# Denominators in the score banks, V's copies on VectorE and no moving product: one edit to the forward recurrence of a fused training step

## The chip, the cores and the metric

The program runs on one core of a Trainium2 chip. The core has a matrix engine (TensorE, in the profile "PE" for its products and "PEld" for its weight loads), a vector engine (VectorE, "DVE"), a scalar engine (ScalarE, "ACT"), GpSimd ("POOL") and SyncE ("SP"), which here only issues DMAs. Each engine works through its own list of instructions in order; semaphores hold an instruction back until what it needs is there. Sums of the matrix engine land in PSUM, which this kernel uses as eight banks; everything else lives in SBUF, or in the chip's memory, which DMAs reach.

The metric is the device time of one execution in microseconds. Before the edit it is 3096.96 us, the median of three runs (3095.86 to 3097.39).

## The reference

The kernel computes a transformer block and all its gradients. The part that matters here is the forward pass of the attention, which is a recurrence over 64 segments of 32 rows: eight memory rows go in front of each segment, and the first eight rows of a segment's output are the memory of the next.

```python
for s in range(n_seg):                       # 64 segments, one after the other
    h = jnp.concatenate([mem, xs], axis=1)   # 8 + 32 rows of 512
    q = jnp.einsum('btd,dhe->bhte', h, Wq)   # 32 heads of 128
    k = jnp.einsum('btd,dhe->bhte', h, Wk)
    v = jnp.einsum('btd,dhe->bhte', h, Wv)
    scores = jnp.einsum('bhqe,bhke->bhqk', q, k) * scale
    scores = jnp.where(mask[None, None], scores, -1000000000.0)
    p = _softmax(scores, axis=-1)
    o = jnp.einsum('bhqk,bhke->bhqe', p, v)
    o = jnp.einsum('bhte,hed->btd', o, Wo)
    mem = o[:, :M, :].copy()                 # the next segment needs it
    outs.append(o[:, M:, :])
```

Around it stand layer norms with a modulation, a gated feed-forward part, and `jax.vjp` over the whole.

## The kernel before, in words

`phase2` is the forward recurrence, a Python loop over `s` from 0 to 63 that writes out one step for each segment. Everything in it is put in the order in which it is traced: `self.pin` at the end of the phase ties each instruction to the one before it on its engine, so the order of the lines is the order on every engine. The backward pass, the feed-forward part and the weight gradients follow in other phases and are not touched.

Three heads are worked on at once: their 3 x 40 rows make 120 columns of a 128-wide group, and 32 heads make `G` = 11 groups. Groups go in three parts of four, four and three (`PG` = 4): "part 0, 1, 2".

A step goes like this:

- `proj` (L692) makes K, Q and V rows of the segment, each in two halves of 16 products of 128x512 (`col_pass`, L255). VectorE copies the first half out of PSUM, ScalarE the second; V's halves are both copied by VectorE, to `RA["v"]`, which is named RA0v in the profile.
- `turns` (L701) transposes K and Q on the matrix engine; VectorE and ScalarE put them head by head into `kT` and `qT`.
- V's rows have to be moved into `Vst`, group by group. Two copies by GpSimd bring the first 1024 columns (L794 for the first half, L797 for the second). The heads of partitions 96 to 127 ("far heads") have to move to partitions 0 to 95. That is `vshift` (L736): three products with a piece of the identity into a bank `sh_ps`, and a VectorE copy from there (L743). V's rows for the memory arrive by DMA from `RBv`, issued by GpSimd a step ahead (`v_tails`, L671).
- `st_exp` (L710) makes the scores of a part in a bank of their own (`st_ps`; the mask was put there before by `mask_mm`, L658), and ScalarE exponentiates them into `ET` (L717).
- `den` (L719) multiplies `ET` with a column of ones: the softmax's denominators. They are put into the unused fourth quarter of the bank `or2`, which later takes part 2 of the output. `recip` (L724) inverts them on VectorE into `rden`, parts 0 and 1 in one instruction, part 2 in another.
- `pv` (L745) multiplies `ET` with `Vst` into `or_ps`. `ost` (L754) scales by `rden` into `Ost`: parts 0 and 2 on VectorE, part 1 on ScalarE in four pieces.
- `ott` (L765) transposes `Ost` on the matrix engine; the copies to `OT` are ScalarE's for parts 0 and 2, VectorE's for part 1.
- `outproj` (L769, products on L223 through `pair_mm`) applies the output weights in 64 products, heads in order, so its first product needs part 0 of `OT` alone. Its sum is split, folded (`at_ft`) and put into the next step's `hT` (L875).

Two of the transposes that the backward pass needs are made by DMA: `VTr` from `Vst` (L814) and `Pst` from `ET` (L820), both on SP's queue, which also carries all stores of rows. At the start of the next step `norm` (L884) scales `Pst` on GpSimd and SP stores `VTr` and `Pst` (L887, L888).

Steps come in fours, since rows of four segments are prepared together. Between the scores and the output a step also holds: in the first of four a modulation product (`mod_ps`, L200), in the second nothing, in the third the transpose of the prepared K rows (`turn_ps`, L618), in the fourth that of the Q rows and a transpose of new input rows (`p1tp`, L415, with a ScalarE copy `hx`, L417). In the text these are the "mod", "plain", "k-turn" and "q-turn" steps. Each step also puts three `mask_mm` of the next step among its transposes.

PSUM has two pools: three banks for `st_ps`, five for everything else ("p").

Of the kernel before, what the change touches and what calls it, by code (L numbers as in the profile page):

```python
# [40 lines left out]
class K:  # L41
# [392 lines left out]
    def phase2(self):  # L434
# [4 lines left out]
        PG = 4  # L439
# [8 lines left out]
        with ExitStack() as ctx:  # L448
# [232 lines left out]
            for s in range(NS):  # L681
# [27 lines left out]

                def st_exp(pi):  # L710
                    st_ps = masked.pop(pi)
# [7 lines left out]
                def den(pi, ps):  # L719
                    for g in range(pi * PG, min(pi * PG + PG, G)):  # L720
                        nc.tensor.matmul(ps[:, PG - 1, g:g + 1], lhsT=ET[:, g * GW:(g + 1) * GW], rhs=self.ones[:, 0:1],
                                         start=True, stop=True)

                def recip(a, b, ps):  # L724
                    a, b = a * PG, min(b * PG, G)
                    nc.vector.reciprocal(rden[:, a:b], ps[0:120, PG - 1, a:b])
# [9 lines left out]
                def vshift():  # L736
                    sh = ps_f32("sh_ps")
                    shf = sh[:].rearrange("p g x -> p (g x)")
                    for hl in range(3):
                        nc.tensor.matmul(shf[32 * hl:32 * hl + 32, 0:384], lhsT=self.ident[96:128, 96:128],  # L740
                                         rhs=RA["v"][96:128, 384 * hl:384 * hl + 384], start=True, stop=True,
                                         tile_position=(96, 32 * hl))
                    nc.vector.tensor_copy(Vst[0:96, 1024:1408], shf[0:96, 0:384])  # L743

                def pv(pi, or_ps=None):  # L745
                    or_ps = or_ps or ps_f32("or_ps")
# [7 lines left out]
                def ost(pi, or_ps, eng):  # L754
                    n = min(PG, G - pi * PG)
                    if eng == "act":
                        for j in range(n):
# [4 lines left out]
                    nc.vector.tensor_tensor(part3(Ost, pi)[0:120, 0:n, :], or_ps[0:120, 0:n, :],  # L762
                                            rden[:, pi * PG:pi * PG + n].unsqueeze(2).to_broadcast([120, n, 128]), op=ALU.mult)

                def ott(pi):  # L765
                    ps, n = transposes_part(Ost, pi)
                    self.evac("dve" if pi == 1 else "act", part3(OT, pi)[:, 0:n, :], ps)
# [9 lines left out]
                if s < NS - 1 and norms:  # L777
                    norms.pop()()
                proj("k", 0, "dve")
                proj("k", 1, "act")  # L780
                if s == NS - 1:
                    nc.gpsimd.dma_start(self.w_gate, io["B_w_gate"].rearrange("(c p) f -> p c f", p=128))
                    norms.pop()()
# [11 lines left out]
                turns()  # L795
                proj("v", 1, "dve")
                nc.gpsimd.tensor_copy(Vst[0:96, 512:1024], RA["v"][0:96, 512:1024])  # L797
# [13 lines left out]
                vshift()  # L811
                st_exp(2)
                if s < NS - 1:
                    nc.sync.dma_start(VTr[:], Vst[:, :], transpose=True)  # L814
                or2 = ps_f32("or_ps")
                den(0, or2)
                or0 = pv(0)
                Pst = sb2.tile([128, G, 128], BF16, name="Pst", bufs=1)
                if s < NS - 1:
                    nc.sync.dma_start(Pst[:], ET[:, :], transpose=True)  # L820
                else:
                    nc.gpsimd.dma_start(self.w_up, io["B_w_up"].rearrange("(c p) f -> p c f", p=128))
                    nc.gpsimd.dma_start(self.w_down, io["B_w_down"].rearrange("(fc p) d -> p fc d", p=128))
                den(1, or2)
                or1 = pv(1)
                recip(0, 2, or2)
                ost(0, or0, "dve")
                ost(1, or1, "act")
                pv(2, or2)
                den(2, or2)  # L830
# [1307 lines left out]
```

The softmax here doesn't subtract the row's maximum and nothing guards it: scores larger than these inputs give would overflow.

## Time and profile before

| | |
|---|---|
| time, median of 3 runs | 3096.96 us |
| the profiled execution | 3095.76 us, of which its span is 3093.9 us |
| forward recurrence | its hand-over copies to the next step (L875) run from 62.8 to 980.5 us of the span |
| one step (from one `at_ft` to the next) | mod 15.04, plain 14.59, k-turn 14.70, q-turn 14.93 us; 14.82 us on average |
| TensorE's granted clock | 0.991; 1.00 in the recurrence |

How to read it: the page gives each engine's busy time and the chain of work that ended last. A step is best read in the timeline of one window: its columns are the start in us, the length in us, the engine, the line, the operation, output <- input, how often, and in brackets how long the engine was idle before and on what it waited. Instructions of one line that stand together are drawn as one row. Products are pipelined and their ends are modelled, so their lengths overlap, and a busy matrix engine says little.

### The profile page before, as it was taken

How to read it: one execution, taken by the hardware profiler on the slowest of the kernel's cores; microseconds unless marked ns; L12 is line 12 of the kernel's file. 1: busy time of each engine (PE TensorE's matmuls, PEld its weight loads, DVE VectorE, ACT ScalarE, POOL GpSimd, SP SyncE). 2: the span in 40 equal slices, each digit the busy share in tenths (PEclk: the TensorE clock that was granted, in tenths of full speed). 3: DMA queues.
4: the chain of work that ended last, by engine and by line, in shares of the span. 5: the costliest groups of instructions: out<-in, count | busy, mean ns of one | idle time of the engine just before them, and what ended most of it. 6: DMA issues, size and time to landing. Idle time of an engine off the chain costs nothing.

```text
span 3093.9 us, 106049 instructions
## 1 busy us (share of the span) xinstructions
PE 2997.4 (97%) x43769; PEld 1835.7 (59%) x43845; DVE 1628.3 (53%) x3799; ACT 1269.5 (41%) x3056; POOL 1378.6 (45%) x2958
## 2 busy tenths in 40 slices
PE   5999999999999899989999999999999999999999
PEld 3666666666665444445577777777777754445454
DVE  4556656665555788742255555555555642322221
ACT  2555555555555433322255555555555530111011
POOL 3666766666766222211244444444444422333322
PEclk8999999999999899999999999999999999999999
DMA  9887788788788799997599999999999998666574
GB/s 299 217 213 203 205 206 216 201 213 211 206 201 255 200 231 232 224 284 247 170 239 243 245 243 244 239 248 244 244 240 245 245 271 279 195 201 220 190 237 148
DMA packets 845944, 703.54 MB, mean 227 GB/s; under 512 B 544306, under 2 KB 717906, under 8 KB 845076
## 3 DMA queue, kind: packets, MB, share of 16 engines
q1 hardware_dynamic: 714148, 486.69, 62.3%
q0 software_dynamic: 60656, 148.64, 14.9%
q10 hardware_dynamic: 70656, 61.41, 6.4%
q8 instruction: 345, 5.65, 0.8%
q14 instruction: 139, 1.14, 0.1%
HBM read 294.93 MB, written 276.35 MB: 185 GB/s over the span
## 4 chain that ended last, share of the span: by engine, by line
PE 90%; DMA 4%; DVE 3%; issue 1%; POOL 1%; ACT 1%; SPq 0%; another core or an unknown queue 0%; DVEq 0%; POOLq 0%; ACTq 0%
PE pass_ps L255 18%; PE gps L1928 13%; PE dh_ps L215 8%; PE g_ps L1590 6%; PE gps5o L1942 4%; PE at_ps L223 4%; PE dhq_ps L223 4%; PE gps L1277 3%; PE mm L1121 3%; PE dh_tps L215 3%; PE turn_ps L264 2%; PE dp_ps L1569 2%; PE tps L1502 2%; PE tps L733 2%; PE mm L1081 2%; DVE RA0v L63 1%
## 5 line engine op out<-in xcount | busy, mean ns | idle before, releaser
L1928 PE MATMUL gps<-rows,hrows 128*128 128x512 bf16 (+2 forms) x2124 | 415.6, 355 | 1.9
L1928 PEld LDWEIGHTS <-hrows 128*128 128x128 bf16 x2160 | 211.2, 98 | 204.6
L255 PEld LDWEIGHTS <-hT 128*32 128x32 bf16 x6144 | 158.2, 97 | 161.3 <-issue 1.9
L1634 POOL COPY dOst<-RAd 96x512 bf16<-96x512 bf16 x128 | 75.4, 612 | 312.2 <-DVE RAd L63 312.2
L63 DVE CAST ot<-gps 128x512 bf16<-128x512 f32 (+3 forms) x76 | 48.1, 633 | 274.8 <-PE gps L1928 185.8
L1932 POOL DMA_DIRECT2D out_dram<-ot x108 | 81.3, 753 | 248.9 <-DVE ot L63 136.5
L61 ACT ACTIVATE ot<-gps 128x512 bf16<-128x512 f32 (+3 forms) x75 | 41.3, 551 | 349.5 <-PE gps L1928 221.7
L885 POOL TENSOR_TENSOR Pst<-Pst,rden 120x1408 bf16<-120x1408 bf16 x63 | 159.6, 2533 | 43.8 <-issue 28.4
L61 ACT ACTIVATE dVT<-g_ps 128x512 bf16<-128x512 f32 (+1 forms) x192 | 109.5, 570 | 95.3 <-PE g_ps L1590 95.0
L63 DVE CAST RA0v<-pass_ps 128x512 bf16<-128x512 f32 x128 | 88.5, 692 | 89.4 <-PE pass_ps L255 85.5
L215 PE MATMUL dh_ps<-WvT,dVT 128*32 128x512 bf16 x2048 | 133.4, 380 | 0.2 <-DVE RBd L63 0.2
L255 PE MATMUL pass_ps<-Wv,hT 128*32 128x512 bf16 x2048 | 133.3, 380 | 0.0
L1942 PE MATMUL gps5o<-WoT,rows 128*128 128x512 bf16 x580 | 127.8, 379 | 3.9 <-DMA rows<-OSR 3.2
L255 PE MATMUL pass_ps<-Wk,hT 128*32 128x512 bf16 x2048 | 123.3, 383 | 1.5 <-ACT hT L875 1.1
L1579 DVE SCALAR_TENSOR_TENSOR dS<-dp_ps,Pst_l 128x512 bf16<-128x512 f32 (+1 forms) x192 | 112.1, 640 | 22.1 <-PE dp_ps L1577 22.1
L223 PE MATMUL at_ps<-Wo,OT 128*32 128x256 bf16 x4096 | 123.5, 273 | 0.1
L255 PE MATMUL pass_ps<-WoT,dyT 128*32 128x256 bf16 (+1 forms) x3072 | 122.4, 308 | 0.9 <-ACT dyT L1708 0.9
L223 PE MATMUL dhq_ps<-WqT,dQT 128*32 128x256 bf16 x4096 | 122.9, 273 | 0.0
L215 PE MATMUL dh_ps<-WkT,dKT 128*32 128x512 bf16 x2048 | 122.2, 380 | 0.0
L255 PE MATMUL pass_ps<-Wq,hT 128*32 128x512 bf16 x2048 | 121.6, 379 | 0.0
L223 PEld LDWEIGHTS <-dQT 128*32 128x32 bf16 x4096 | 109.6, 97 | 15.9
L717 ACT ACTIVATE ET<-st_ps 128x480 bf16<-128x480 f32 (+1 forms) x192 | 96.0, 535 | 42.6 <-ACT qT L61 34.7
(419 smaller groups left out, 7082.2 us busy)
## 6 DMA issues: line engine op xcount, KB each, us to landing
OSR<-Ost SPq DMA_DIRECT2D x64, 352.0 KB
OT<-OT SPq DMA_DIRECT2D x64, 352.0 KB
VT<-VTr SPq DMA_DIRECT2D x64, 352.0 KB
PS<-Pst SPq DMA_DIRECT2D x64, 352.0 KB
OT_l<-OT SPq DMA_DIRECT2D x64, 352.0 KB
Pst_l<-PS SPq DMA_DIRECT2D x64, 352.0 KB
VT_l<-VT SPq DMA_DIRECT2D x64, 352.0 KB
DVR<-rows_x POOLq DMA_DIRECT2D x64, 352.0 KB, 6.4
```

The lines of the kernel that those rows point to most:

```text
L61: return nc.scalar.activation(out, in_, AF.Copy)
L63: return nc.vector.tensor_copy(out, in_)
L215: self.nc.tensor.matmul(ps[32 * j:32 * j + 32, :], lhsT=lhsT, rhs=w, start=(n < 4), stop=(n >= total - 4), tile_position=(0, 32 * j))
L223: nc.tensor.matmul(ps[32 * j:32 * j + 32, :], lhsT=x[k], rhs=w[k][:, 256 * d:256 * d + 256], start=(n == 0), stop=(n == total - 1), tile_p ...
L255: self.nc.tensor.matmul(ps[32 * j:32 * j + 32, :], lhsT=lhs(c), rhs=rhs, start=(c == 0), stop=(c == DC - 1), tile_position=(0, 32 * j))
L717: nc.scalar.activation(part3(ET, pi)[:, 0:n, 0:120], st_ps[:, 0:n, 0:120], AF.Exp, scale=cfg.scale)
L885: nc.gpsimd.tensor_tensor(Pst[0:120, :, :], Pst[0:120, :, :], rden[:, :].unsqueeze(2).to_broadcast([120, G, 128]), op=ALU.mult)
L1121: nc.tensor.matmul(hp[:], lhsT=xT[:, fc, :], rhs=wT[:, fc, :], start=(n == 0), stop=(n == 2 * FC - 1))
L1579: nc.vector.scalar_tensor_tensor(out=part3(dS, pi), in0=ps[:, 0:n, :], scalar=cfg.scale, in1=part3(Pst, pi), op0=ALU.mult, op1=ALU.mult)
L1590: nc.tensor.matmul(ps[:, j, :], lhsT=lh[:, g * GW:(g + 1) * GW], rhs=rh[:, g * GW:(g + 1) * GW], start=True, stop=True)
L1928: nc.tensor.matmul(ps[:, 0:ng * E], lhsT=hrows[:, tp_, c * 128:(c + 1) * 128], rhs=rows[:, tp_, 0:ng * E], start=(tp_ == 0), stop=(tp_ == ...
L1942: nc.tensor.matmul(pss[gg][:], lhsT=src[0][:, src[1], gg * E:(gg + 1) * E], rhs=dyrows[:, tp_, :], start=(tp_ == order[0]), stop=(tp_ == o ...
```

## The change: what it does

1. The denominators of part `pi` are written into columns 120 to 123 of that part's own score bank, which the scores leave free, instead of into `or2`. `recip` becomes three instructions, one for each part, and the next step's `mask_mm` of a bank now follows it.
2. `vshift` is removed. Its place is taken by `far`, which copies V's far heads directly from `RA["v"][96:128]` on VectorE: two copies (32x384 and 32x128) after the first half of V, two (32x256 each) after the second.
3. The copy of V's second half into `Vst` moves from GpSimd to VectorE.
4. The DMA transpose of `ET` to `Pst` is issued ahead of that of `Vst` to `VTr`; both stand behind part 0 of `pv`.
5. The modulation product and the transposes of the prepared rows are put between the scores and the first `den`.
6. `ost` of part 0 is cut into two VectorE instructions of two groups, around `recip` and `ost` of part 1. `OT` of parts 0 and 2 is copied by VectorE, of part 1 by ScalarE, and the three `mask_mm` stand around part 0's transpose.
7. In the last step `norm` is put behind V's copies; the store of `Pst` is returned as a function of its own and is called at once.

The diff, cut to its core:

```diff
-                def den(pi, ps):
+                def den(pi):
                     for g in range(pi * PG, min(pi * PG + PG, G)):
-                        nc.tensor.matmul(ps[:, PG - 1, g:g + 1], lhsT=ET[:, g * GW:(g + 1) * GW], rhs=self.ones[:, 0:1],
+                        j = 120 + g - pi * PG
+                        nc.tensor.matmul(sts[pi][:, 0, j:j + 1], lhsT=ET[:, g * GW:(g + 1) * GW], rhs=self.ones[:, 0:1],
                                          start=True, stop=True)
-                def recip(a, b, ps):
-                    a, b = a * PG, min(b * PG, G)
-                    nc.vector.reciprocal(rden[:, a:b], ps[0:120, PG - 1, a:b])
+                def recip(pi):
+                    a, n = pi * PG, min(PG, G - pi * PG)
+                    nc.vector.reciprocal(rden[:, a:a + n], sts[pi][0:120, 0, 120:120 + n])
...
-                def vshift():
-                    sh = ps_f32("sh_ps")
-                    shf = sh[:].rearrange("p g x -> p (g x)")
+                def far(hf, engs):
                     for hl in range(3):
-                        nc.tensor.matmul(shf[32 * hl:32 * hl + 32, 0:384], lhsT=self.ident[96:128, 96:128],
-                                         rhs=RA["v"][96:128, 384 * hl:384 * hl + 384], start=True, stop=True,
-                                         tile_position=(96, 32 * hl))
-                    nc.vector.tensor_copy(Vst[0:96, 1024:1408], shf[0:96, 0:384])
+                        lo, hi = max(384 * hl, 512 * hf), min(384 * hl + 384, 512 * hf + 512)
+                        if lo < hi:
+                            self.evac(engs.pop(0), Vst[32 * hl:32 * hl + 32, 1024 + lo - 384 * hl:1024 + hi - 384 * hl],
+                                      RA["v"][96:128, lo:hi])
...
                 turns()
+                far(0, ["dve", "dve"])
                 proj("v", 1, "dve")
-                nc.gpsimd.tensor_copy(Vst[0:96, 512:1024], RA["v"][0:96, 512:1024])
+                nc.vector.tensor_copy(Vst[0:96, 512:1024], RA["v"][0:96, 512:1024])
+                far(1, ["dve", "dve"])
+                if s == NS - 1:
+                    norms.pop()()()
...
                 st_exp(0)
                 st_exp(1)
-                vshift()
                 st_exp(2)
-                if s < NS - 1:
-                    nc.sync.dma_start(VTr[:], Vst[:, :], transpose=True)
-                or2 = ps_f32("or_ps")
-                den(0, or2)
-                or0 = pv(0)
...
-                den(1, or2)
-                or1 = pv(1)
-                recip(0, 2, or2)
-                ost(0, or0, "dve")
-                ost(1, or1, "act")
-                pv(2, or2)
-                den(2, or2)
-                recip(2, 3, or2)
-                ost(2, or2, "dve")
...
                 fill(s4, "turn")
+                den(0)
+                or0 = pv(0)
+                Pst = sb2.tile([128, G, 128], BF16, name="Pst", bufs=1)
+                if s < NS - 1:
+                    nc.sync.dma_start(Pst[:], ET[:, :], transpose=True)
+                    nc.sync.dma_start(VTr[:], Vst[:, :], transpose=True)
...
+                recip(0)
+                ost(0, or0, "dve", 0, 2)
+                den(1)
+                or1 = pv(1)
+                recip(1)
+                ost(1, or1, "act")
+                ost(0, or0, "dve", 2, 4)
                 if s4 == 3:
                     p1(s // nseg_t + P1_AHEAD, 4)
...
+                den(2)
+                or2 = pv(2)
+                recip(2)
+                ost(2, or2, "dve")
                 if more:
                     mask_mm(more.pop(0))
+                ott(0, "dve")()
+                while more:
+                    mask_mm(more.pop(0))
+                o1 = ott(1, "act")
+                o2 = ott(2, "dve")
+                o1()
+                o2()
```

## The prediction, made before the changed kernel was run

> **What bounds the kernel now.** I read the page first for its shares, then the chain of waits through the recurrence, then the timeline of single steps. The page alone would say that the matrix engine is all there is:
>
> ```profile
> PE 2997.4 (97%) x43769; PEld 1835.7 (59%) x43845; DVE 1628.3 (53%) x3799; ACT 1269.5 (41%) x3056; POOL 1378.6 (45%) x2958
> ```
>
> The chain of waits in a plain step shows where the time between V's last product and the output products goes (start, length, what):
>
> ```profile
> 604.13 0.70 DVE RA0v L63
> 604.84 0.04 issue
> 604.88 0.34 PE sh_ps L740 x2
> 605.22 0.26 PE st_ps L715 x3
> 605.48 0.08 PE or_ps L721 x4
> ...
> 605.92 0.22 DVE rden L726
> ...
> 608.19 1.87 PE at_ps L223 x64
> ```
>
> The matrix engine stands still while VectorE copies V's second half, because two products of `vshift` and then the scores of part 2 stand behind that copy. From the start of that copy (I call it e0) to the first output product this step takes 608.19 - 604.13 = 4.06 us. The same two pieces give 4.51 in the mod step (648.62 to 653.13), 4.18 in a k-turn step (678.25 to 682.43) and 4.34 in a q-turn step (633.70 to 638.04). Only this stretch is changed; the rest of a step (10.5 us) is left as it is. The timeline shows who is late in it:
>
> ```profile
> 603.54 0.28 DVE L63 COPY qT<-turn_ps 128x64 bf16<-128x64 bf16 x2
> 604.13 0.69 DVE L63 CAST RA0v<-pass_ps 128x512 bf16<-128x512 f32 x1 [0.31 <-PE pass_ps L255]
> 604.41 1.63 ACT L717 ACTIVATE ET<-st_ps 128x480 bf16<-128x480 f32 x3 [0.55 <-ACT qT L61]
> ...
> 605.25 0.55 DVE L743 CAST Vst<-sh_ps 96x384 bf16<-96x384 f32 x1 [0.42 <-PE sh_ps L740]
> ...
> 605.92 0.21 DVE L726 RECIPROCAL rden<-or_ps 120x8 f32<-120x8 f32 x1
> 606.16 0.69 DVE L762 TENSOR_TENSOR Ost<-or_ps,rden 120x512 bf16<-120x512 f32 x1
> 606.29 1.14 ACT L759 ACTIVATE Ost<-or_ps,rden 120x128 bf16<-120x128 f32 x4 [0.25 <-PE or_ps L750]
> ```
>
> ScalarE's exponentials end at 606.04 whatever the matrix engine does (three in a row, from 604.41). Its scaling of part 1 starts at 606.29, ends at 607.43, and the transposes of parts 1 and 2 and the output follow from there. So the quantity to follow is: when does ScalarE start the scaling of part 1? Now the matrix engine sets it, by 0.25 us.
>
> **What the skill says.** Four places, the last of them with the cost that it bears on. *Trainium Kernel Development and Optimization*, section Performance Expectations: matmul busy time is a bad metric of how near the roofline a kernel is. The trace agrees: 97% on the page beside the standstill above. *VectorE: DVE Perf Modes*, The perf-mode tier table: a copy from SBUF to SBUF in bf16 runs at four elements a cycle. The trace has such copies (L277): 1536 columns 0.556 us, 1024 columns 0.421 us, so 0.26 ns a column and 0.156 us fixed. The same page, Two Vector instructions with no wait between them: an instruction whose input or output starts in another group of 32 partitions than that of the one before is held until all earlier ones have finished. The trace agrees where partitions 96 and 0 alternate:
>
> ```profile
> 1000.93 0.69 DVE L897 TENSOR_TENSOR Pst<-tps,rden 120x512 bf16<-120x512 bf16 x1
> 1001.65 0.43 DVE L896 COPY Pst<-tps 32x512 bf16<-32x512 bf16 x1
> 1002.12 0.69 DVE L897 TENSOR_TENSOR Pst<-tps,rden 120x512 bf16<-120x512 bf16 x1
> ```
>
> Each starts 0.03 us after the end of the one before, while instructions on the same partitions overlap (the three of L277 at 28.10 take 1.36 us together, 1.53 one by one: 0.085 us overlap).
>
> **The change part by part**, in the plain step above.
>
> *Out:* `vshift`'s products and the standstill. The scores of part 2 follow those of part 1 at once, some 0.8 us earlier. But exponentials are paced by ScalarE (604.41 to 606.04) and start with part 0, so no `ET` comes earlier. L743's 0.55 us on VectorE and L797's 0.61 on GpSimd go. GpSimd's time is free here: its Vst DMAs come earlier and are for the next step. So this edit alone gives the matrix engine time, and 0.25 us of it can be used before ScalarE's scaling.
>
> *In, on VectorE.* Each of the new copies changes its group of 32 partitions in input or output, so I take no overlap and 0.03 us between two. V's copies to the first reciprocal, with the fit above for copies: the far copies of the first half start at 603.85, behind qT: 0.255 and 0.19, to 604.32. V's second half is thus copied from 604.35 (now 604.13) to 605.04; `Vst` 0.29 to 605.36; two far copies of 0.22 to 605.86; reciprocal of part 0 (0.17, as L726 on three columns) to 606.06; half of `ost` part 0, 256 columns: L762 takes 0.691 for 512 and 0.557 for 384, so 0.42, from 606.09 to 606.52; the reciprocal of part 1 begins 0.08 before that ends, as L726 does now at 606.77, and ends at 606.61. ScalarE starts at 606.66 instead of 606.29. **VectorE is 0.37 us later than the matrix engine was.** It ends part 1 at 607.80.
>
> *Behind it.* Now the mask products, and ScalarE's copy of part 0, which waits behind the scaling, delay the output products to 608.19, 0.76 after the scaling's end. After, masks and turns are done by then, part 0 is copied by VectorE (second half of `ost` to about 606.95, reciprocal, part 2 to 607.63, copy 0.42 to 607.97), and only one transpose of part 1, three of part 2 and one or two others follow: 0.06 to start, then 0.067 us each (four weight loads take 0.27 at 607.49), and the first output product at about 608.31. Part 1's copy on ScalarE (608.2 to 608.8) is needed after 24 of 64 products, at 608.31 + 0.70, so it is hidden.
>
> By kind of step, from e0 as it is now:
> - plain: 608.31 - 604.13 = 4.18, now 4.06: **+0.12**;
> - k-turn: one transpose (`ao_b_tp`) fewer, the turn now lies beside the exponentials: 4.12, now 4.18: **-0.06**;
> - q-turn: the same, but ScalarE's `hx` (0.61) runs behind the scaling and the program makes the output's bank wait for it: 608.44, 4.33, now 4.34: **0**;
> - mod: the output's bank is the one that ScalarE's copy of part 1 frees in this order of buffers, so the first output product waits for that copy: 608.2 + 0.60 + 0.05, 4.75, now 4.51: **+0.24**.
>
> Together +0.30 us in four steps, 0.075 a step, in 63 steps **+4.7 us**.
>
> *The other edits.* Three reciprocals for two, and two halves of `ost`, are in the sum. SP: the transpose of `ET` can go at 606.1 instead of 607.43, that of `Vst` at about 607.7 instead of 605.88. The store of `VTr` (L887) waits for the latter to land; it may now wait some 2 us. Behind it stand the store of `Pst`, which waits for GpSimd anyway (at 600.54 in this step, 5.6 us after L887), and K's and Q's rows, which have a buffer for each second step: hidden. Cover gone, SP would be late by 2 us in 14.8, without anybody waiting before the next Ost. GpSimd's `norm` gets its data earlier. In the last step `norm` (2.53 us) stands ahead of two weight loads (w_up from 988.68 to about 989.2) and SP's loads for the next phase stand behind the store of `Pst`: between 0 and 2.8 us, I take 0.5.
>
> A cost the trace doesn't show: VectorE's new copies run beside GpSimd's DMA issues (L675, L676, 0.51 us each), which now stand there. *SBUF — State Buffer*, SBUF: two separate sides, says that such a copy and GpSimd exclude one another. Below: 0; L404 (SBUF to SBUF) at 608.45 began while L676 ran (608.01, 0.51) and L653 began within it, and all took their usual length (0.54, 0.51, 0.50). Above: each of five copies waits half an issue, 0.25 us. I take 0.
>
> Sum: +4.7 + 0.5 = +5.2. The profiled execution (span 3093.9, 1.86 outside it, 3095.76) lies 1.2 below the median 3096.96; I add to the median: **3102 us**. From the bounds of its terms (0.1 us a step in the row on VectorE, 6 us; the end, 0 to 2.8) this case reaches from 3094 to 3110.
>
> **The rivals.**
> - *VectorE's row is shorter* (faster). If the seven new boundaries overlap as on equal partitions (0.115 us each), the reciprocal of part 1 is ready before the exponentials end; ScalarE starts at 606.1, 0.56 earlier than in my sum: 0.56 - 0.075 = 0.485 a step, 30 us: 3067. Half of that: 3082. For it: L743 and the standstill really go. Against it: L896 and L897.
> - *GpSimd and VectorE shut each other out* (slower, the other side of 3097). From 0.1 us a copy on, the five copies add 0.5 us a step, 31 us: 3133; on top of the sum above 0.01 us a copy (3 us) is enough to pass 0.2%. For it: the page on SBUF. Against it: L404.
> - *The matrix engine's freed time counts in full*: 0.7 us a step, 44 us, 3053. Against it: exponentials and scaling are ScalarE's and VectorE's. I count it with the first.
>
> **How the numbers follow.** Main case 0.6, at 3102. The faster rivals 0.25, the slower one 0.15. About 0.2% (6.2 us) is what a measurement of this kernel can tell from no change: 3090.8 to 3103.2. The main case lies in it with 0.34, above it with 0.24, below it with 0.02. Faster 0.27, same 0.34, slower 0.39. The range takes in the half-way case of the first rival and part of the second: 3077 to 3123.
>
> **What would show it.** Right: in the plain step ScalarE's scaling of part 1 released by a reciprocal and no longer by the matrix engine, starting about 2.5 us after V's second copy would have started (now 2.16); VectorE without a gap from kT to that reciprocal; copies of 0.29, 0.255, 0.22 and 0.19; in the mod step the first `at_ps` product right behind ScalarE's `OT`. Steps of about 15.3, 14.7, 14.65 and 14.9 us. Wrong: ScalarE's scaling right behind the exponentials and steps of 14.4 us (overlap), or copies of 0.4 us and more (GpSimd).

## The result, and the profile after

The changed kernel takes 3116.93 us (median of 8 runs, 3112.38 to 3123.06), the kernel before in the same comparison 3097.39 us (8 runs, 3095.86 to 3109.07). The ratio is 1.0059 with a 95% interval of 1.0045 to 1.0073: slower by 0.6%, or 19.5 us. The prediction had 3102, with a range of 3077 to 3123.

The page of the changed kernel says as little as that of the kernel before did:

```profile
PE 2997.5 (96%) x43653; PEld 1831.3 (59%) x43653; DVE 1690.6 (54%) x4247; ACT 1235.6 (40%) x2992; POOL 1339.5 (43%) x2894
```

VectorE is busy 62 us longer, GpSimd 39 us less. On VectorE the copies of V within SBUF add 78 us and the copy of `OT`'s part 2 adds 23; the copy behind `vshift` took 35, which are gone. The split reciprocals and scalings add 18, and some of all this overlaps. Where the time went is found by setting the two traces side by side (steps counted from 0), from one first output product (`at_ps`) to the next, and up to the first product of the feed-forward part (`mm`), behind which nothing was edited:

| stretch | before, us | after, us | difference |
|---|---|---|---|
| start to the output of step 1 | 74.05 | 76.98 | +2.9 |
| output of step 1 to output of step 62 (61 steps) | 903.23 | 915.13 | +11.9 |
| the last step | 14.00 | 17.17 | +3.2 |
| last output's start to the feed-forward's first product | 28.29 | 29.97 | +1.7 |
| the rest, unchanged code | 2074.33 | 2076.80 | +2.5 |

The two profiled executions differ by 22.1 us, the medians by 19.5. The last line is scatter: in eleven other profiles of this study (all but far_late) it lies between 2073.06 and 2078.49 us. The first and the fourth line scatter as well: with the same first step as here swap12 has 74.46 us, and with the same last step mod_alone has 31.43 us from the last output to the feed-forward. The lines of the 61 steps and of the last step hold: profiles that share the code there agree within 0.2 us. In the 61 steps a regular mod, plain, k-turn and q-turn step takes 15.45, 14.84, 14.79 and 14.94 us, which is +0.41, +0.24, +0.09 and +0.01.

The plain step that the prediction worked with looks like this in the timeline of the changed kernel (start, length, engine, line, what):

```profile
613.03 0.45 DVE L63 COPY Vst<-RA0v 32x384 bf16<-32x384 bf16 x2
...
613.52 0.69 DVE L63 CAST RA0v<-pass_ps 128x512 bf16<-128x512 f32 x1
613.60 1.40 ACT L719 ACTIVATE ET<-st_ps 128x480 bf16<-128x480 f32 x3 [0.55 <-ACT qT L61]
...
614.25 0.29 DVE L799 COPY Vst<-RA0v 96x512 bf16<-96x512 bf16 x1
...
614.57 0.45 DVE L63 COPY Vst<-RA0v 32x256 bf16<-32x256 bf16 x2
...
615.05 0.18 DVE L729 RECIPROCAL rden<-st_ps 120x4 f32<-120x4 f32 x1
...
615.32 0.42 DVE L763 TENSOR_TENSOR Ost<-or_ps,rden 120x256 bf16<-120x256 f32 x1
...
615.66 0.17 DVE L729 RECIPROCAL rden<-st_ps 120x4 f32<-120x4 f32 x1
615.75 0.39 DVE L763 TENSOR_TENSOR Ost<-or_ps,rden 120x256 bf16<-120x256 f32 x1
...
615.92 1.14 ACT L760 ACTIVATE Ost<-or_ps,rden 120x128 bf16<-120x128 f32 x4 [0.93 <-PE or_ps L751]
616.06 0.17 DVE L729 RECIPROCAL rden<-st_ps 120x3 f32<-120x3 f32 x1
...
616.34 0.56 DVE L763 TENSOR_TENSOR Ost<-or_ps,rden 120x384 bf16<-120x384 f32 x1
...
617.56 1.93 PE L223 MATMUL at_ps<-Wo,OT 128*32 128x256 bf16 x64
```

ScalarE's exponentials (613.60) end at 615.00 and it then stands for 0.93 us. The bracket names the matrix engine, but its products of part 1 are done at 615.2; the last thing that the scaling needs is the second reciprocal, which ends at 615.83. The row on VectorE is as the prediction wrote it down, with one difference: behind each of the two reciprocals there is a gap of 0.09 us before the instruction that uses it, on VectorE (615.23 to 615.32) and on ScalarE (615.83 to 615.92). In the kernel before, VectorE's gap there is 0.03 us in every step. Why it grew is not shown.

The last step shows something else. The timeline there:

```profile
1001.56 2.54 POOL L884 TENSOR_TENSOR Pst<-Pst,rden 120x1408 bf16<-120x1408 bf16 x1
...
1001.93 2.48 DVE L63 COPY Vst<-RA0v 32x384 bf16<-32x384 bf16 x2
...
1004.44 0.69 DVE L63 CAST RA0v<-pass_ps 128x512 bf16<-128x512 f32 x1
...
1004.84 1.09 POOL L832 DMA_DIRECT2D Wv<-in_B_w_down_dram  x1
1005.17 0.89 DVE L799 COPY Vst<-RA0v 96x512 bf16<-96x512 bf16 x1
...
1006.11 0.61 PE L751 MATMUL or_ps<-Vst,ET 128*128 128x128 bf16 x4 [2.29 <-DVE Vst L799]
...
1009.29 3.42 PE L223 MATMUL at_ps<-Wo,OT 128*32 128x256 bf16 x64
```

Two far copies that take 0.45 us in a plain step take 2.48, and they end just behind GpSimd's multiplication (`norm`, 1001.56 to 1004.10). The matrix engine stands for 2.29 us, and then works at half speed: its 64 output products take 3.42 us for 1.93. Stretch by stretch (window, its length, busy time and count of the matrix engine, granted clock, then the share and GB/s of the DMAs):

```profile
1006.00:1009.00 3.00, 2.67 (x21) 0.50 0.94 241
1009.00:1013.00 4.00, 4.00 (x80) 0.58 0.97 352
1013.00:1018.00 5.00, 4.31 (x81) 1.00 1.04 374
```

In the kernel before, the stretch from 989 to 993 us, its last step, has a clock of 1.00.

### The profile page after: what moved, and what is told of

It is laid out like the page before. It is cut to its first block, busy times and chain, and to the rows that moved or that the text cites. A ratio compares the mean times of both kernels' runs of the same rounds, so it can differ in the third digit from the quotient of the medians.

```text
span 3116.1 us, 106220 instructions
## 1 busy us (share of the span) xinstructions
PE 2997.5 (96%) x43653; PEld 1831.3 (59%) x43653; DVE 1690.6 (54%) x4247; ACT 1235.6 (40%) x2992; POOL 1339.5 (43%) x2894
## 4 chain that ended last, share of the span: by engine, by line
PE 60%; issue 4%; DMA 3%; POOL 1%; DVE 1%; ACT 1%; SPq 0%; POOLq 0%; ACTq 0%; DVEq 0%
PE gps L1927 9%; PE dh_ps L215 8%; PE g_ps L1589 6%; PE pass_ps L255 5%; PE gps5o L1941 4%; PE dhq_ps L223 4%; PE gps L1276 3%; PE mm L1120 3%; PE dh_tps L215 3%; PE dp_ps L1568 2%; PE tps L1501 2%; PE mm L1080 2%; PE mm L1095 1%; PE mm L1053 1%; PE mm L1057 1%
## 5 line engine op out<-in xcount | busy, mean ns | idle before, releaser
L310 DVE TENSOR_TENSOR dST<-dh_ps,dST 128x512 bf16<-128x512 f32 x64 | 44.3, 692 | 130.8 <-ACT dST L309 130.8
```

## The experiments

Labels in brackets. "Scaling" is ScalarE's scaling of part 1; its start and that of the first output product are counted from the start of V's second copy out of PSUM, which in the changed kernel is itself 0.20 us later in the step than before (2.18 instead of 1.98 us behind V's first copy). No run undoes the new place of the denominators (item 1), of the prepared rows' work (item 5) or the split of `ost` (item 6) alone; what these are worth is not known.

### First and last step put back [ends]

```diff
                 if s == NS - 1:
                     nc.gpsimd.dma_start(self.w_gate, io["B_w_gate"].rearrange("(c p) f -> p c f", p=128))
+                    norms.pop()()()
...
                 proj("v", 1, "dve")
+                if s == 0:
+                    for f in firsts["v"]:
+                        f()
                 nc.vector.tensor_copy(Vst[0:96, 512:1024], RA["v"][0:96, 512:1024])
                 far(1, ["dve", "dve"])
-                if s == NS - 1:
-                    norms.pop()()()
                 if s == 0:
-                    for f in firsts["v"]:
-                        f()
                     v_tails(0)
```

> Two places of the changed kernel are put back, both outside the regular steps: the last step's norm on GpSimd goes back ahead of V's copies, and in the first step the copies of the prepared V rows go ahead of VectorE's new copies. Theory (GpSimd's multiplication keeps VectorE's far copy of the last step waiting for 2.0 us, and the matrix engine's clock halves after each standstill): the last step falls from 17.2 to about 14.3 us, the far copy from 2.28 to 0.25 us, the half-clock stretch of the last step goes; with the first step 5 to 7 us in all, so 13 to 15 us over the kernel before. Rival (the last step is late because its weight loads and stores moved): the last step stays above 16.5 us, and the whole gains less than 2 us.

Measured: 3111.88 us, 14.1 over the kernel before (ratio 1.0041, interval 1.0028 to 1.0054). The last step takes 14.49 us, the output products 1.93, and the output of step 1 starts at 73.88 instead of 76.98 us; the 61 steps between are unchanged (915.16). The feed-forward starts 6.2 us earlier than in the changed kernel. `norm`'s place and its meeting with VectorE's copies are thus shown to cost 2.7 of the last step's 3.2 us; of the 1.7 us behind it, 0.5 come back, which is within the scatter. The far copy of 384 columns takes 0.47 us here and not the 0.25 of the theory.

The first step is another matter. VectorE's copies did delay the copy of the prepared V rows `RBv`: it starts 3.78 instead of 2.84 us behind V's first copy. GpSimd's DMAs of these rows start at 52.36 instead of 51.42, and the first product of part 0 at 56.90 instead of 56.14, but 0.47 us of this lateness are there at V's first copy, ahead of any edited instruction. What lies behind that standstill is a stretch at half clock, and it is of two lengths. These are the kernel before, the changed kernel, swap12 (the same first step) and far_pool_mod (the first step put back), each in two windows:

```profile
55.60:59.00 3.40, 2.86 (x27) 0.50 0.29 81
59.00:62.40 3.40, 3.36 (x91) 1.00 1.43 170
...
56.60:60.00 3.40, 2.75 (x25) 0.51 0.61 113
60.00:63.40 3.40, 3.40 (x53) 0.50 1.11 279
...
56.00:59.40 3.40, 3.17 (x28) 0.50 0.28 69
59.40:62.80 3.40, 3.40 (x95) 1.00 1.36 180
...
54.20:57.60 3.40, 1.70 (x19) 0.50 0.41 128
57.60:61.00 3.40, 3.40 (x42) 0.50 0.75 156
```

In the changed kernel the longer stretch reaches into the output products of step 0 (3.05 for 1.93 us); swap12 has the short one and is only 0.4 us behind the kernel before at the output of step 1 (74.46), and far_pool_mod has the long one although its first step is put back. So of the 2.9 us about 0.4 is left as the edit's own; 0.5 lies ahead of it, and the rest goes with the length of that stretch, which the order in the first step does not settle. For the same reason the 3.1 us that this run gains there are not the order's alone.

### norm's place alone, in the kernel before [norm_before]

```diff
-                    norms.pop()()
...
                 nc.gpsimd.tensor_copy(Vst[0:96, 512:1024], RA["v"][0:96, 512:1024])
+                if s == NS - 1:
+                    norms.pop()()
```

> The kernel before, with one edit alone: the last step's norm on GpSimd is put behind V's copies, where the change has it. Theory (the last step of the changed kernel is lost because VectorE's copies from SBUF to SBUF are shut out while GpSimd multiplies): here VectorE reads PSUM at that time, so nothing waits; the last step stays at 14.0 us (within 0.3), no half-clock stretch before the output products, the time within 2 us of the kernel before. Rival (norm's place costs by itself, through the weight loads and stores behind it): the last step is 2 us or more longer, the time 3 to 5 us over the kernel before.

Measured: 3102.37 us, 4.5 over the kernel before (1.0019, 1.0012 to 1.0026). Each theory has half of it. The last step is 14.00 us, to the hundredth that of the kernel before: where VectorE copies out of PSUM, the multiplication on GpSimd holds nobody. So the standstill of 2.3 us in the changed kernel comes not from the place of `norm` alone but from its meeting with copies from SBUF to SBUF. The 4.5 us are lost later. The timeline:

```profile
988.71 2.53 POOL L886 TENSOR_TENSOR Pst<-Pst,rden 120x1408 bf16<-120x1408 bf16 x1
...
991.27 0.32 SPq L889 DMA_DIRECT2D PS<-Pst  x1
...
994.25 6.49 SPq L930 DMA_DIRECT2D Wv<-AOA  x4
...
1025.33 1.68 PE L1055 MATMUL mm<-Wk,hdT 128*128 128x448 bf16 x4 [16.70 <-DMA hdT<-h]
```

SP's store of `Pst` waits for `norm`, and the loads of the next phase stand behind it on SP: the loads from `AOA` begin at 994.25 instead of 989.50, and the feed-forward's first product at 1025.33 instead of 1019.57. In the changed kernel the same loads begin at 1008.51, 0.8 us ahead of its last output (before: 1.8 us ahead, here 3.0 us behind it), so there the late output covers most of it.

### Two engines ready at the same moment [mix]

```diff
-                nc.vector.tensor_copy(Vst[0:96, 512:1024], RA["v"][0:96, 512:1024])
+                nc.gpsimd.tensor_copy(Vst[0:96, 512:1024], RA["v"][0:96, 512:1024])
```

> The changed kernel with V's second half copied by GpSimd again; the far copies stay on VectorE, so that a VectorE copy and a GpSimd copy become ready at the same moment in each step. Theory that the two engines shut each other out: one of the two shows its wait in every step (VectorE's first far copy some 0.7 instead of 0.22 us, or GpSimd's copy some 0.85 to 1.05 instead of 0.61), and the step gains nothing (0 to 0.3 us longer, 0 to 20 us over the changed kernel). Theory that they run side by side, as the copies do beside GpSimd's short DMA issues: 0.22 and 0.61 us, VectorE's row 0.3 us shorter, some 18 us under the changed kernel, level with the kernel before.

Measured: 3118.94 us (1.0063, 1.0050 to 1.0076), and regular steps as in the changed kernel to 0.01 us. VectorE's row lost an instruction of 0.29 us, and the scaling still starts 2.40 us behind V's second copy. The timeline of the plain step:

```profile
612.45 0.77 DVE L63 COPY Vst<-RA0v 32x256 bf16<-32x256 bf16 x2
612.48 0.67 POOL L799 COPY Vst<-RA0v 96x512 bf16<-96x512 bf16 x1 [1.57 <-DVE RA0v L63]
...
613.26 0.18 DVE L729 RECIPROCAL rden<-st_ps 120x4 f32<-120x4 f32 x1
```

The two far copies take 0.77 instead of 0.45 us, GpSimd's copy 0.67 instead of 0.61. One by one, VectorE's first far copy keeps its 0.22 us, GpSimd's copy is 0.06 longer, and VectorE's second takes 0.54 and ends 0.07 us behind GpSimd's (613.22 and 613.15). It is so in every regular step. Shutting out is shown, for an elementwise instruction on GpSimd against a VectorE copy within SBUF.

### The far copies behind the reciprocal of part 1 [far_late, far_late2]

```diff
-                far(1, ["dve", "dve"])
...
                 recip(1)
                 ost(1, or1, "act")
+                far(1, ["dve", "dve"])
```

> The changed kernel with the two far copies of V's second half moved behind the reciprocal of part 1; nothing else. Theory (VectorE's row ahead of the reciprocal of part 1 sets ScalarE's scaling, and this the output products): ScalarE's scaling starts 0.4 to 0.45 us earlier after V's second copy (1.95 to 2.0 instead of 2.40), the output products 0.3 us earlier in a step, 0.4 in a mod step; some 20 us in all, so about level with the kernel before (-5 to +3 us). Rival (VectorE's row as a whole, up to its copy of OT's part 0, is full, or the matrix engine's list decides): less than 5 us gained, 15 to 19 us over the kernel before.

Measured: 3568.66 us (1.1516, 1.1501 to 1.1532), which answers nothing of the question. The DMA that transposes `Vst` stood ahead of the moved copies in the program, so `VTr` got the far columns of two steps earlier, and the copies waited for that DMA. In the view of waits VectorE stands 343.0 us ahead of these copies, in 63 steps, until that DMA has read `Vst`. With that DMA moved along:

> The changed kernel with the two far copies of V's second half moved behind the reciprocal of part 1, and the DMA that transposes Vst behind them in program order (in the run far_late it stood ahead of them, so that it took the far columns of two steps earlier and the copies waited for it). Theory (VectorE's row ahead of the reciprocal of part 1 sets ScalarE's scaling, and this the output products): ScalarE's scaling starts 0.4 us earlier after V's second copy (2.0 instead of 2.40), the output products 0.3 us earlier in a step, 0.4 in a mod step; some 20 us, so -5 to +3 us to the kernel before. Rival (VectorE's row as a whole, up to its copy of OT's part 0, is full, or the matrix engine's list decides): less than 5 us gained, 15 to 19 us over the kernel before.

Measured: 3115.22 us (1.0061, 1.0049 to 1.0074), 17.3 over the kernel before: the rival's case. The 61 steps gain 2.4 us (912.71), where some 20 were forecast. Its timeline, in a plain step where V's second copy starts at 671.48:

```profile
673.37 0.46 DVE L63 COPY Vst<-RA0v 32x256 bf16<-32x256 bf16 x2
673.42 1.14 ACT L760 ACTIVATE Ost<-or_ps,rden 120x128 bf16<-120x128 f32 x4 [0.47 <-PE st_ps L724]
...
673.88 0.33 PE L751 MATMUL or_ps<-Vst,ET 128*128 128x128 bf16 x3 [0.64 <-DVE Vst L63]
...
674.47 0.56 DVE L763 TENSOR_TENSOR Ost<-or_ps,rden 120x384 bf16<-120x384 f32 x1
...
675.47 1.71 PE L223 MATMUL at_ps<-Wo,OT 128*32 128x256 bf16 x56
```

The scaling starts 1.94 us after V's copy instead of 2.40, as the theory has it, and the first output product at 3.99 instead of 4.04. The copies now hold the products of part 2 (0.64 us), VectorE scales part 2 to 3.55 instead of 3.38, and its transposes stand ahead of the output on the matrix engine. In the changed kernel part 2 is scaled 0.16 us ahead of the end of ScalarE's part 1 (616.90 and 617.06): both ways were nearly equally long. What counts is VectorE's row as a whole, not the place of one instruction in it.

### All of V's copies on GpSimd [v_pool]

```diff
-                far(0, ["dve", "dve"])
+                far(0, ["pool", "pool"])
...
-                nc.vector.tensor_copy(Vst[0:96, 512:1024], RA["v"][0:96, 512:1024])
-                far(1, ["dve", "dve"])
+                nc.gpsimd.tensor_copy(Vst[0:96, 512:1024], RA["v"][0:96, 512:1024])
+                far(1, ["pool", "pool"])
```

> The changed kernel with all five copies of V that VectorE was given (two far copies after each half, V's second half) on GpSimd, ahead of its DMAs for the next step. Theory (VectorE's row is the bound): V's second copy out of PSUM starts 0.2 us earlier, ScalarE's scaling some 0.4 us earlier than that again, the output products 0.45 us earlier in a step; 25 us in all, so 5 to 10 us under the kernel before. Rival (GpSimd's slower copies hold the products of part 1 and 2 back): products of part 2 0.5 us later than now, and the time at or over that of the changed kernel.

Measured: 3098.35 us (1.0002, 0.9994 to 1.0011), level with the kernel before, where 5 to 10 us under it were forecast. The regular steps did what the theory says: scaling 0.45 us earlier (0.20 + 0.25), 14.51, 14.46 and 14.47 us for plain, k-turn and q-turn, mod 15.12; the 61 steps take 898.77, 4.5 under the kernel before. Two things took it back. In a few steps GpSimd's longer list is late (16.49, 16.21 and 15.37 us in three of them, where products of the output's parts wait 1.08, 0.91 and 0.40 us for its copies), and in the last step `norm` stands behind V's copies, as in norm_before: from the last output to the feed-forward 35.79 us, 7.5 more than before. And the timeline of a regular step shows what is next:

```profile
603.41 0.83 POOL L65 COPY Vst<-RA0v 32x256 bf16<-32x256 bf16 x2
...
604.29 0.33 PE L751 MATMUL or_ps<-Vst,ET 128*128 128x128 bf16 x3 [0.42 <-POOL Vst L65]
```

Products of part 2 wait 0.42 us for GpSimd's far copies, which stand behind its copy of V's half.

### The mod step [swap12, mod_alone]

```diff
-                o1 = ott(1, "act")
-                o2 = ott(2, "dve")
+                o1 = ott(1, "dve")
+                o2 = ott(2, "act")
```

> The changed kernel with OT's part 1 copied by VectorE and part 2 by ScalarE. Theory (in the mod step the output's bank is the one that the copy of part 1 frees): VectorE's copy takes 0.42 for ScalarE's 0.60 us and begins 0.1 us earlier, so the mod step is 0.25 to 0.35 us shorter, the other steps change by less than 0.05; 16 such steps, 4 to 5 us under the changed kernel. Rival (ScalarE's scaling of part 1 and the transposes end just as late): the mod step changes by less than 0.1 us.

Measured: 3116.59 us (1.0059, 1.0043 to 1.0075), mod step 15.51. The timeline of a mod step:

```profile
659.56 0.42 DVE L63 COPY OT<-tps 128x512 bf16<-128x512 bf16 x1 [0.15 <-PE tps L736]
...
659.87 0.49 ACT L61 ACTIVATE OT<-tps 128x384 bf16<-128x384 bf16 x1 [0.63 <-PE tps L736]
...
660.41 1.93 PE L223 MATMUL at_ps<-Wo,OT 128*32 128x256 bf16 x64 [0.46 <-ACT OT L61]
```

The wait went along with ScalarE: the output now waits for ScalarE's copy of part 2. Which copy it waits for is thus not a property of the part. What can make the mod step differ is its own bank: `mod_ps` is written ahead of the output products and read by ScalarE behind the output (L205), so one of five banks is missing all that time. The other experiment removes that:

```diff
                 or0 = pv(0)
+                if mod_row:
+                    mod_row()
...
                 evac_turned()
-                if mod_row:
-                    mod_row()
```

> The changed kernel with one edit: ScalarE takes the row of the modulation product out of its bank right behind part 0 of the output products, not behind the output. Theory (in a mod step this product keeps one of the five banks until after the output, and so the output gets a bank that ScalarE's copy of OT has just left): the mod step falls from 15.45 to 15.0 to 15.1 us, the others stay; 6 us in 16 steps, 13 us over the kernel before. Rival (another wait as late as that one, ScalarE's scaling 0.25 us later behind the row): the mod step changes by less than 0.1 us.

Measured: 3106.70 us, 8.9 over the kernel before (1.0034, 1.0021 to 1.0048); mod step 14.98, the others as they were; the 61 steps take 907.62 instead of 915.13. In its timeline the output starts before ScalarE's copy of part 1 has ended:

```profile
653.85 0.25 ACT L205 ACTIVATE modrow<-mod_ps 1x128 f32<-1x128 f32 x1
...
656.51 0.60 ACT L61 ACTIVATE OT<-tps 128x512 bf16<-128x512 bf16 x1 [0.46 <-PE tps L736]
...
656.69 1.93 PE L223 MATMUL at_ps<-Wo,OT 128*32 128x256 bf16 x64
```

So this one wait is worth 7.5 us in the 61 steps: 6.6 in the fifteen mod steps and 1.2 in step 7, a q-turn step that also holds a modulation product; the others take 0.2 back. The change had lost 5.9 of its 11.9 us in these steps, so they are now even a little shorter than before; the other 6.0 us stay, in the plain and the k-turn steps.

### The moving product back in [vshift]

```diff
-                far(0, ["dve", "dve"])
-                nc.vector.tensor_copy(Vst[0:96, 512:1024], RA["v"][0:96, 512:1024])
-                far(1, ["dve", "dve"])
+                nc.gpsimd.tensor_copy(Vst[0:96, 512:1024], RA["v"][0:96, 512:1024])
...
+                vshift()
                 st_exp(2)
```

> The changed kernel with the moving product back in place of the far copies (its three products before the scores of part 2, one VectorE copy of 0.55 us from the bank) and V's second half copied by GpSimd; denominators, order of the DMAs, split scaling and copies of OT stay as changed. Theory (what counts is the length of VectorE's row up to the reciprocal of part 1, by 0.55 us here and by 1.36 with the copies): V's second copy starts 0.2 us earlier, ScalarE's scaling about 2.55 us after it, which is 0.05 to 0.1 us earlier than in the changed kernel; 11 to 19 us over the kernel before. Rival (the far copies are what cost, and the rest of the change gains): level with the kernel before or under it.

Measured: 3127.15 us, 29 over the kernel before (1.0098, 1.0084 to 1.0111); neither theory has that. In the plain step the theory holds: scaling at 2.45 us, step 14.68. In k-turn, q-turn and mod steps it starts at 2.85, 2.85 and 3.06. There the transposes of the prepared rows, or the modulation product, lie between the scores and the denominators. The timeline of such a step:

```profile
634.14 0.74 PE L743 MATMUL sh_ps<-RA0v,ident 32*32 32x384 bf16 x3
...
634.98 0.61 PE L618 MATMUL turn_ps<-ident,RBk 128*128 128x128 bf16 x8
635.43 0.24 PE L724 MATMUL st_ps<-ones,ET 128*128 128x1 bf16 x4
```

With the standstill of the moving product ahead of them, they push the denominators out to 1.35 us behind the start of the exponentials (634.08), for 0.62 in the changed kernel (613.60 to 614.22), whose k-turn and q-turn steps start the scaling as early as the plain one. So the new place of that work (item 5 of the change) costs as long as the product is there (item 2); whether it gains anything without it, no run shows.

### Put together [pool_swap_ends, far_pool_mod, far_pool_mod_vtr]

v_pool, swap12 and ends in one kernel:

> V's copies on GpSimd (as v_pool), OT's parts 1 and 2 exchanged (as swap12), first and last step put back (as ends). If the three causes add up: mod step 14.8 us, the others 14.46, the last step 13.8, no half-clock stretch in it, 7 to 12 us under the kernel before. If GpSimd's longer queue takes back what the row on VectorE gives: within 3 us of the kernel before.

Measured: 3094.41 us, 3.5 under the kernel before (0.9987, 0.9980 to 0.9993). The causes did not add up as told: the mod step is 15.19, since swap12 gains nothing; the last step takes 13.81. Then, with what mod_alone and v_pool's wait suggest:

```diff
-                far(0, ["dve", "dve"])
+                far(0, ["pool", "pool"])
                 proj("v", 1, "dve")
...
-                far(1, ["dve", "dve"])
...
                 nc.vector.tensor_copy(Vst[0:96, 512:1024], RA["v"][0:96, 512:1024])
+                far(1, ["pool", "pool"])
...
                 or0 = pv(0)
+                if mod_row:
+                    mod_row()
...
                 evac_turned()
-                if mod_row:
-                    mod_row()
```

> The far copies on GpSimd, V's second half on VectorE as in the changed kernel, the row of the modulation product taken out of its bank right behind part 0 of the output products instead of behind the output, first and last step put back. In v_pool the products of part 2 waited for GpSimd's last far copy. Theory: VectorE's copy (0.29 us) starts first, GpSimd's far copies follow 0.3 us later and end 0.3 us earlier than in v_pool; plain, k-turn and q-turn steps 14.2 to 14.35 instead of 14.46, and in the mod step the output's bank no longer waits for ScalarE: 14.5 to 14.7 instead of 15.12. In all 14 to 22 us under the kernel before. Rival (ScalarE's scaling and the transposes hold the three regular steps at 14.46): only the mod step gains, 8 to 12 us under the kernel before. If GpSimd starts first, VectorE's copy takes 0.6 to 0.8 us and the regular steps are at 14.6 or more.

Measured: 3079.02 us, 19.9 under the kernel before (0.9935, 0.9922 to 0.9947). The mod, plain, k-turn and q-turn steps take 14.65, 14.38, 14.33 and 14.48 us. The total is as forecast; the q-turn step has gained nothing on v_pool's 14.47, as its rival had it, and the plain step lies a little over the forecast 14.35. The timeline:

```profile
593.78 0.29 DVE L803 COPY Vst<-RA0v 96x512 bf16<-96x512 bf16 x1
...
593.81 0.96 POOL L65 COPY Vst<-RA0v 32x256 bf16<-32x256 bf16 x2 [0.47 <-DMA QST<-RA1q]
```

VectorE starts first and keeps its 0.29 us, and GpSimd pays 0.13 us of waiting (0.96 for 0.83), and no product waits for it in this step. The same with the two DMA transpositions in their old order (item 4 of the change undone):

> As far_pool_mod, but with the DMA transposition of Vst ahead of that of ET again. Theory (GpSimd's loads of the next V rows wait for the transposition of Vst, so each one that comes late leaves GpSimd late in the step after): the odd steps over 15 us beyond the mod steps go, 1 to 4 us under far_pool_mod. Rival (ET's transposition then waits for GpSimd's far copies, and norm and with it V's copies of the next step come late): 0 to 10 us over far_pool_mod. If the order of the two is of no account: within 1.5 us.

Measured: 3078.02 us (0.9929, 0.9915 to 0.9942). The regular steps are the same; one odd step of 15.45 us is gone. The intervals of the two overlap, so whether the order is worth the 1 us stays open. Both are faster than the kernel before and than the changed one.

## Why the prediction was right, and where not

*The side and the range* were right: slower, 3116.9 in 3077 to 3123. The main case's own size was not: +5.2 was forecast, its bounds ended at 3110, and +19.5 was measured. That 3116.9 lies in the range is in part luck: the range goes up to 3123 for the sake of the rival in which GpSimd and VectorE shut each other out in every step. That happened in no regular step, and other items filled the place.

*VectorE's row in the plain step* was right in all its durations: copies of 0.25, 0.19, 0.29 and 0.22 us, halves of 0.42 and 0.39, V's second copy 0.20 us later (0.22 said). ScalarE's scaling starts 2.60 us after e0 where the prediction has 2.53. The two gaps behind reciprocals, 0.09 us each for the 0.03 and 0.05 of the sum, add 0.10; V's second copy, 0.02 earlier than said, takes some back.

*The differences by kind* were +0.12, -0.06, 0 and +0.24 for plain, k-turn, q-turn and mod, and came out as +0.24, +0.09, +0.01 and +0.41. The step that failed here is where the prediction took its baseline. It read 4.06, 4.18 and 4.51 us from the chain of waits, whose piece starts at 608.19 in the plain step; the first output product starts at 608.13 in the timeline. Against a baseline of 4.00, its own 4.18 is +0.18. With the later scaling this closes the plain and the k-turn step. In the q-turn step the two views differ by 0.01 only (638.04 and 638.02), and the sum came out right because two errors cancel: the scaling is 0.07 later, but `hx` starts 0.12 us ahead of the scaling's end (646.57 and 646.69), as it does before, where the sum had it behind. Two sums are also off by a little as they stand: 608.44 - 604.13 is 4.31 and not 4.33, and 608.2 + 0.60 + 0.05 lies 4.72 behind 604.13 and not 4.75. In 61 steps the change was to cost 4.6 us and cost 11.9; the baselines, 0.05 us a step, are 3.2 of the difference.

*The mod step's bank* was named rightly, as a wait of the output for ScalarE's copy of part 1, and mod_alone shows that it is the largest single item, 7.5 us. It was undersized (0.24 for 0.41; 0.07 of this is the baseline). What swap12 adds is that the cure is not in that copy but in the bank that the modulation product keeps.

*"When does ScalarE start the scaling of part 1?"* was too narrow a question. far_late2 starts it 0.46 us earlier and gains 2.4 us in 61 steps; v_pool shortens the whole row and the regular steps fall by 0.33 us and more. So VectorE's row is what the change lost in the regular steps, and it is shown by taking the row away.

*The other edits, "I take 0.5", at most 2.8* is the step that failed most: it was 3.2 us in the last step alone, of which `ends` brings 2.7 back, and 1.7 behind it, which is not clear of the scatter. The prediction followed `norm` along GpSimd and SP, where norm_before shows a cost of 4.5 us, and did not ask what VectorE would do beside it. The 2.9 us at the start had no term at all, and the first step's `RBv` copy was not followed along VectorE's list; but only some 0.4 of them is shown to be the edit's, and the rest is the length of the half-clock stretch and the lateness ahead of it.

*GpSimd against VectorE* was taken as 0 for the short DMA issues, and that was right: of some 300 copies of V on VectorE beside issues of `v_tails`, none is longer than elsewhere by more than 0.01 us, but for one that also stood beside a GpSimd copy. The evidence given for it, L404 beside a DMA issue, says nothing of a multiplication. *SBUF — State Buffer*, SBUF: two separate sides, says that whichever starts first keeps the shared ports for its whole instruction; the last step agrees (2.28 us for one copy of 0.25), and so does VectorE's second far copy in mix. GpSimd's copy there does not quite: it starts 0.03 us behind VectorE's first copy of 0.22 us and is only 0.06 us longer. The lock thus struck where an elementwise instruction of GpSimd stood beside the copy, and the rival that had every copy wait in every step did not come.

*The faster rivals* did not come: the boundaries between copies do not overlap (613.03 to 615.02 is without a gap of more than 0.04 us), and the matrix engine's freed time was not used.

## What to carry to other kernels

When instructions are moved, look along every engine that will then be busy at the same moment, in the first and the last turn of the loop too: in these runs a copy within SBUF on VectorE was held until the elementwise instruction on GpSimd that had started ahead of it was done. When the next wait is less than 0.2 us behind, taking away the last one gains little; shorten the row that all the waits share. And take the baseline and the forecast from the same view, since 0.05 us a step between two views is 3 us in 61 steps. And before a difference ahead of or behind the loop is put down to an edit, look whether another run with the same code there has it too.

## What the runs showed of the hardware that was not expected

- A standstill of the matrix engine of 2.3 us was enough to halve its clock for 6.8 us: it is at 0.50 from 1005.6 to 1012.4 us, and 64 output products take 3.42 for 1.93 us. *TensorE: Matmul & The Clock Gate*, Part 1: The HAM clock gate, puts the switch at about one idle window of 3.4 us; here less was enough, for in the 3.41 us ahead of 1005.56 the engine had worked 1.33 us. In all traces here the half-clock stretches last a multiple of 3.41 us, so that work that ends a little earlier or later can pay for one window more. The share of a window that settles it is not shown: 2.90 of 3.40 us of work ended the half clock in `ends` (55.3 to 58.7), and 3.13 did not in swap12 (1004.9 to 1008.3).
- Some long DMA issues on GpSimd held a VectorE copy. L799 took 0.89 for 0.29 us and ended 0.13 us after the issue of 1.09 us beside it (1004.84), and it took 0.88 to 0.89 in far_late2, swap12 and mod_alone too; in `ends` a far copy took 0.47 for 0.25 us and ended 0.04 us after an issue of 0.80. These copies began 0.32 to 0.38 us into the issue. Copies that began 0.07 us into the one (`ends`, 999.34) and 0.19 into the other (changed kernel, 1004.23) took their usual 0.19. The issues of 0.5 us never held one.
- The time from the end of a reciprocal to VectorE's next instruction that uses it was 0.03 us in the kernel before and 0.09 to 0.10 in the changed one. Nothing here shows why.
